# New landing times and durations in a list scheduler's plan, with a third buffer for one tile, in an attention and mixture kernel

## The chip, the cores and the metric

The kernel runs on one core of a Trainium2 chip. TensorE (PE) does the matrix products, ScalarE (ACT) and VectorE (DVE) the elementwise work, SyncE (SP) issues every transfer. The metric is the time of one execution on the device in microseconds, the median of several runs.

## What is computed

```python
def _attn_ref(q, k, v, cap):                      # q, k, v: 4 x 12 heads x 448 x 64
    scores = matmul(q, k.T) / sqrt(64)
    scores = cap * tanh(scores / cap)             # cap = 30
    attn = exp(scores - max)
    attn = attn / (sum(attn) + 1e-09)
    return attn @ v
def _moe_ref(x, w1, w2, w3, w_out):               # x: 1792 x 768, weights in float64
    a = x @ w1
    b = x @ w2
    return (a * b @ w3) @ w_out                   # 768 -> 1024 -> 1024 -> 768
```

The attention's result, its heads laid side by side, is the x of the second part.

## The kernel before

**Attention.** The 48 heads are taken as 24 pairs (`pr`), 128 keys at a time. `plan_S` multiplies q and k on TensorE, ScalarE takes the tanh (L486) and the exp (L489) of 128x896 elements in place in a tile `p`. `plan_V` multiplies `p` with v (L526, L541) into one of two PSUM banks, and `plan_X` adds up the exps for the denominator: for the pairs in `ADDS` (L365) VectorE first adds the tiles of p (L591, L593) and TensorE sums one tile (L608); for the other pairs TensorE sums three. Then ScalarE copies the product out of PSUM into a tile `xf` (task `O`, L674), which frees the bank; the sums go through four transfers and a reciprocal (`R0` L678, `R1`, `R2` L687, `R3` L691), VectorE multiplies `xf` by the result (`N0`, L714), and SyncE stores `xf` to `x_dr` (`N`, L717). The tile `xf` has two buffers in the pool `smp`, so the copy of pair pr waits for the store of pair pr - 2.

**Weights.** They come in float64. A piece of 128x384 is loaded as pairs of words (`raw_w`, `raw_wo`, three buffers, L238), and `Piece` makes a float32 of it: `top` on ScalarE (L253) or VectorE (L246), `low` (L258), `sign` (L261) and `join` (L266) on VectorE. A high and a low part are split off (L272, L275, L313, L316), and each product is made of three passes. `plan_wo`, `plan_w3` and `plan_C` make w3 times w_out (`pc`, L1175) while the attention runs; `plan_W` makes the seven combinations of w1 and w2 that a scheme with seven block products instead of eight needs, and stores them (`w_dr`), since they are read again for the second half of the tokens.

**The second part.** `plan_xprep(r)` loads x for half r of the tokens and makes its combinations (`xs`, tiles `x0B`, `x0T`, `x1B`, `x1T`). `plan_moe(r, m)` multiplies them in eight rounds m (`pab`, L1040), with copies out of PSUM named M1, U, M5 and V (L1009) and sums (L1020), and stores a * b to `u_dr`. Round m of half 0 runs beside the attention from about 210 us on. `plan_out` multiplies the result with w3 times w_out (`m`, L1394).

**What sets the order.** Each `put` adds a task with its engine (and sometimes a second one that may take it), its planned duration, a due time (`key`), the tasks it needs and a `lat`, the time from the issue of a transfer to its landing. `Plan.run` (L94) walks through planned time: for the engine that is free first it takes, of the tasks whose needs are met by then, the one with the smallest due time, and emits its instructions. Loads with `spare` are held back by `SPARE`, 2500 ns more. So these numbers do not change what is computed; they set the order of the instructions on each engine, and which of two engines does a conversion. On the chip each engine then runs its instructions strictly in that order and waits at each one for its operands.

Of the kernel before, what the change touches and what calls it, by code (L numbers as in the profile page):

```python
# [148 lines left out]
def program(  # L149
# [127 lines left out]
    def plan_piece(nm, x, key, lead, first=(), whole=True):  # L277

        n = x.n / PC
        for st, eng, ns, fn, needs, lat, alt in (  # L280
            ("load", "SP", 450, lambda: x.load((rawp, rtp)), (), 3300, ()),
            ("low", "DVE", 75 + 200 * n, x.low, ("load",), 0, ()),
            ("sign", "DVE", 75 + 400 * n, x.sign, ("low",), 0, ()),
            (
                "top", "DVE", 75 + 200 * n, lambda: x.top((rawp, rtp)), ("load",), 0,
                [("ACT", 140 + 272 * n, lambda: x.top_a((rawp, rtp)))] * TOPA,
            ),
            ("join", "DVE", 75 + 400 * n, x.join, ("top", "sign"), 0, ()),
            (
                "high", "ACT", 140 + 272 * n, lambda: x.high_out(nc.scalar.copy), ("join",), 0,  # L290
                [("DVE", 75 + 200 * n, lambda: x.high_out(nc.vector.tensor_copy))],
            ),
            ("out", "DVE", 75 + 400 * n, x.low_out, ("high",), 0, ()),
        )[: 7 if whole else 5]:
            need = [f"{nm}{y}" for y in needs]
            need += list(first) if st == "high" else []
            t = put(f"{nm}{st}", eng, ns, key, fn, need, lat, alt)
            if st == "load":
                t.key -= lead
                t.spare = SPARE  # L300
                raw = plan.tag("raw", NRAW).take(t)
            elif st == "top":
                tt = plan.tag("rt", NRT).take(t)
            if st not in ("high", "out"):
                raw.append(t)
            if st in ("join", "high", "out"):
                tt.append(t)
        return tt
# [53 lines left out]

    LANDS = {0: 3300, 1: 6000, 2: 5000}

    ADDS = [(2,3) if pr>3 else () for pr in range(NPAIR)]  # L365

    def due(pr, i=0):

# [20 lines left out]
    def plan_load(pr):  # L389
        key = due(pr, 0) if pr % 2 else due(pr, 1)  # L390

        def emit():
            raw_t[pr] = qkp.tile([P, QO + KQ], F32, tag="raw", name=f"kq{pr}", bufs=3)
            for c in cuts(pr):
                c = slice(c.start + QO if c.start else 0, (c.stop if c.stop < HK else KQ) + QO)
                nc.sync.dma_start(raw_t[pr][:, c], kq[pr][:, c])

        def emit2():
            v_t[pr] = qkp.tile([P, 7, D], F32, tag="v", name=f"v{pr}")
            nc.sync.dma_start(v_t[pr], v[pr].rearrange("p (m d) -> p m d", m=7))  # L400

        t = put(f"ld{pr}", "SP", 450, key - 12, emit, lat=LANDS.get(pr, 3300))
# [45 lines left out]
    def plan_S(pr, i):  # L448
# [56 lines left out]
        use["p", pr, i] = plan.tag("t" if i else "t0", 5 if i else 2).take(t)  # L505
        if not i:
            use["p", pr + 1, i] = use["p", pr, i]
        t = put(f"E{nm}", "ACT", 935, key, exp, [f"H{nm}"])
        if not i:
            done[f"E{pr + 1}_0"] = t  # L510
        use["p", pr, i].append(t)
# [68 lines left out]
    def plan_X(pr):  # L580
# [89 lines left out]
            nc.scalar.copy(r[0][:, :SH], box[1][:, :SH])  # L670

        def take_values():
            r[1] = smp.tile([P, S], F32, tag="x", name=f"xf{pr}")
            nc.scalar.copy(r[1], pv_t[pr][:, :S])  # L674

        def fold():
# [29 lines left out]
        t = put(f"R2{pr}", "SP", 450, end, unfold, [f"R1{pr}"], 2000)  # L706
        use["z", pr].append(t)
        use["rd", pr] = plan.tag("rd", 2).take(t)
        t = put(f"R3{pr}", "SP", 900, end, spread, [f"R2{pr}"], 2500)
        use["rd", pr].append(t)  # L710
        use["r", pr].append(t)

# [6 lines left out]
        t = put(f"N0{pr}", "DVE", 536, end + 5, scale, [f"R3{pr}", f"O{pr}"])  # L719
        use["r", pr].append(t)  # L720
        use["x", pr].append(t)
        t = put(f"N{pr}", "SP", 450, end + 5, store, [f"N0{pr}"], 2000)
        use["x", pr].append(t)

    def plan_general(pr):

        def emit():
# [47 lines left out]
            for j in range(2):  # L775
                at = slice(j * D, (j + 1) * D)
                for m in range(NCH):
# [5 lines left out]
                        start=(m == 0),  # L783
                        stop=(m == 3),
                    )
            xf = smp.tile([P, S], F32, tag="x", name=f"gx{pr}")
            nc.scalar.copy(xf, pv[:, :S])
            nc.sync.dma_start(x_dr[pr], xf)

# [10 lines left out]

    XORD = (1, 2, 6, 5, 7, 3, 4)
    GATE, NW = 8.0, 4
    RT0, RWIN = (145, 330), (170, 104.0)
    wt, wuse, xt, xuse = {}, {}, {}, {}

    def slot(tag):
# [22 lines left out]
    def plan_W(m):  # L829
# [19 lines left out]
        def split(op, of, needs):  # L849
            i = [x for x in range(7) if LHS[XORD[x]] == op][0]  # L850
            q = m * 7 + i
            j = q // NW
            k = key + 3 + i

            def dst(x):
                if x == 0 and (q, "new") not in wt:
                    wt[q, "new"] = w_new(q)
                return wt[q, "new"][:, x].rearrange("p a b -> p (a b)")

            first = [f"W{(q - q % NW) // 7}_{(q - q % NW) % 7}h"] if q % NW else []  # L860
# [9 lines left out]
            t = put(f"WS{m}_{i}", "SP", 450, k + 4, store, [f"{nm}_{i}l"], 2500)  # L870
            wuse[j].append(t)
            done[f"w0_{m}_{i}"] = done[f"{nm}_{i}l"]

# [17 lines left out]
    def plan_W_again(m):  # L891

        for i in range(7):
            q = (KF + m) * 7 + i

            def load(q=q, i=i):
                nc.sync.dma_start(w_new(q).rearrange("p x a b -> p (x a b)").bitcast(F32), w_dr[m, i])

            p = q - q % NW - KF * 7
            t = put(  # L900
                f"w1_{m}_{i}", "SP", 450, w_key(1, m, i) - 12, load,
                [f"WS{m}_{i}"] + [f"w1_{p // 7}_{p % 7}"] * (q % NW > 0), 3500,
            )
# [11 lines left out]
    def plan_xprep(r):  # L915
# [10 lines left out]
        def load(nm, kt, src, key, needs):  # L926
            x = nm, kt

            def emit():
                tiles[x] = xsp.tile([P, 512], F32, tag="xs", name=f"xs{r}{nm}{kt}")[:, :S]  # L930
                nc.sync.dma_start(tiles[x], src)

            t = put(f"X{r}{nm}{kt}", "SP", 450, key, emit, needs, 2500)
            t.spare = SPARE
            use["xs", r, nm, kt] = plan.tag("xs", NXS).take(t)

# [24 lines left out]
        p0 = r * PH  # L961
        for kt in range(HX):
            a0, b0 = p0 + kt, p0 + HB + kt
            key = max(due(b0, 3) + 14, (140 + 3 * kt) * (r == 0))
            load("a0", kt, x_dr[a0], key - 8, [f"N{a0}"])
            load("b0", kt, x_dr[b0], key - 7, [f"N{b0}"])
            split("B11", "a0", kt, key, [f"X{r}a0{kt}"])
# [3 lines left out]
            def keep(kt=kt):  # L971
                nc.sync.dma_start(t_dr[r, kt], tiles["a0", kt])

            t = put(f"XT{r}{kt}", "SP", 450, key, keep, [f"X{r}T1{kt}"], 2000)
            use["xs", r, "a0", kt].append(t)
        for kt in range(HX):
            a1, b1, b0 = p0 + HX + kt, p0 + HB + HX + kt, p0 + HB + kt
            key = max(due(b1, 3) + 14, (140 + 3 * (3 + 2 * kt)) * (r == 0))
# [13 lines left out]
    def plan_moe(r, m):  # L992
# [170 lines left out]
    def plan_C(n):  # L1163

        for nh in range(2):
# [40 lines left out]
            )  # L1206
            o.append(t)
            ev = plan.tag("ev", NEV).take(t)
            ev.append(put(f"DS{n}_{nh}", "SP", 450, key, store, [f"D{n}_{nh}"], 2000))

    def plan_bt(k, late):

# [3 lines left out]
        def load(nm, a, nh):  # L1216
# [50 lines left out]

    def plan_out(t):

        key = K0 + 14.5 * t - 10 * (t == 0)  # L1270
        ru, box, ob = {}, {}, {}

        if t == 4:
# [5 lines left out]
        def load_quadrant(a, b):  # L1279
            nm = f"A{a + 1}{b + 1}"  # L1280

            def load():
# [152 lines left out]
        def store(name, a, nh, need):  # L1435
# [174 lines left out]
```

## Time and profile before

| | |
|---|---|
| Median of 3 runs | 617.76 us (614.71 to 619.55) |
| The profiled execution | 611.22 us, of which the span is 609.3 us |
| TensorE busy | 558.6 us |
| VectorE busy | 449.9 us |
| ScalarE busy | 327.6 us |
| Mean busy share of the 16 DMA engines | 67.5% for the SyncE queue |

The share of a busy engine is an average over stages with different limits. The kernel has four: a start, the attention with the weight conversion beside it (to about 335 us), the preparation of the second half of x (335 to 424 us), and a tail of matrix products (424 us to the end). A row of the timeline gives the start, the duration, the engine, the line, what is written and read, and, in brackets, the idle time before it and what ended it.

### The profile page before, as it was taken

To read this page: it belongs to the slowest core of one execution; us is meant where nothing else is said; L and a number is where in the kernel's file an instruction comes from. 1 tells how busy PE (TensorE), PEld (TensorE's weight loads), DVE (VectorE), ACT (ScalarE), POOL (GpSimd) and SP (SyncE) were. 2 spreads that over 40 slices of the span, in tenths; PEclk is the share of its full clock that TensorE was granted. 3 is DMA by queue.
4 is the path that set the end of the run, shared out by engine and by line. 5 is a ranking of instruction groups with operands and counts; after the bars stand their busy time and mean duration, and the time that the engine had idled before them with its cause. 6 is when DMAs were issued, how large, how long until landed. Compare 5 with 4: busy or idle time off the path is not lost.

```text
span 609.3 us, 9488 instructions
## 1 busy us (share of the span) xinstructions
PE 558.6 (92%) x3340; PEld 429.5 (70%) x3340; DVE 449.9 (74%) x909; ACT 327.6 (54%) x514; POOL 0.2 (0%) x4
## 2 busy tenths in 40 slices
PE   4999999998999599979899599879999999999995
PEld 2445477665576355646568488768999999999995
DVE  5988998796989779698988779777622388878511
ACT  5998986695677587666873343422212152433200
POOL 0000000000000000000000000000000000000000
PEclk9999999999999799989999889999999999999998
DMA  6668775768688665687777975999886653545211
GB/s 226 198 220 249 235 249 179 231 218 266 203 309 273 203 220 165 199 279 220 274 292 248 333 273 213 362 332 352 273 322 238 237 184 125 169 132 152 63 53 58
DMA packets 80089, 137.45 MB, mean 226 GB/s; under 512 B 13602, under 2 KB 53410, under 8 KB 80034
## 3 DMA queue, kind: packets, MB, share of 16 engines
q1 hardware_dynamic: 80034, 136.77, 67.5%
q8 instruction: 28, 0.46, 0.3%
q14 instruction: 27, 0.22, 0.1%
HBM read 91.67 MB, written 44.98 MB: 224 GB/s over the span
## 4 chain that ended last, share of the span: by engine, by line
PE 46%; DMA 27%; DVE 12%; ACT 8%; SPq 3%; issue 3%; DVEq 0%; ACTq 0%
PE pab L1040 18%; PE m L1394 17%; DMA raw_w<-in_moe_w_dram 5%; DMA r_dr<-z 4%; DMA r<-r_dr 4%; DMA c<-cc_dr 4%; PE pc L1175 4%; PE s L473 3%; ACT p L486 3%; DMA x_dr<-xf 3%; DMA raw_wo<-in_moe_w_out_dram 3%; PE pv L526 2%; ACT p L489 2%; DMA z<-r 2%; DVE wt L316 1%
## 5 line engine op out<-in xcount | busy, mean ns | idle before, releaser
L489 ACT ACTIVATE p<-p,ncap_sb,acap_sb 128x896 f32<-128x896 f32 x84 | 92.1, 1141 | 0.0
L486 ACT ACTIVATE p<-s,tsc_sb 128x896 f32<-128x896 f32 x84 | 81.7, 1015 | 8.2 <-PE s L473 7.8
L1175 PEld LDWEIGHTS pc<-wo,w3t 128*128 128x128 f32 x384 | 65.6, 188 | 12.1 <-issue 6.8
L1175 PE MATMUL pc<-wo,w3t 128*128 128x384 f32 x384 | 73.9, 342 | 0.0
L1040 PE MATMUL pab<-x0T,wt 128*128 128x448 f32 x288 | 64.9, 373 | 7.1 <-ACT M L1009 6.1
L526 PE MATMUL pv<-p,v 128*64 128x448 f32 x288 | 65.6, 571 | 5.5 <-ACT p L489 5.1
L473 PE MATMUL s<-hl 64*128 64x448 f32 x432 | 60.5, 403 | 10.7 <-ACT p L486 6.1
L473 PEld LDWEIGHTS s<-hl 64*128 64x128 f32 x432 | 38.7, 194 | 38.6 <-ACT p L486 14.1
L1040 PEld LDWEIGHTS pab<-x0T,wt 128*128 128x128 f32 x288 | 53.5, 190 | 16.3 <-ACT M L1009 6.5
L1040 PE MATMUL pab<-x1T,wt 128*128 128x448 f32 x288 | 61.8, 366 | 2.7 <-DVE M L1020 2.0
L1394 PE MATMUL m<-bT,ot 128*128 128x384 f32 x336 | 60.7, 334 | 0.0
L1040 PEld LDWEIGHTS pab<-x1T,wt 128*128 128x128 f32 x288 | 53.8, 188 | 7.8 <-DVE M L1020 2.4
L1394 PEld LDWEIGHTS m<-bT,ot 128*128 128x128 f32 x336 | 58.5, 188 | 0.0
L1040 PE MATMUL pab<-x0B,wt 128*128 128x448 f32 x216 | 50.7, 381 | 5.0 <-DVE M L1009 2.2
L1040 PEld LDWEIGHTS pab<-x0B,wt 128*128 128x128 f32 x216 | 40.8, 194 | 13.5 <-DVE M L1009 3.4
L1040 PE MATMUL pab<-x1B,wt 128*128 128x448 f32 x216 | 47.5, 368 | 2.6 <-DVE U L1020 1.0
L1394 PE MATMUL m<-bB,ot 128*128 128x384 f32 x252 | 46.1, 334 | 0.0
L1040 PEld LDWEIGHTS pab<-x1B,wt 128*128 128x128 f32 x216 | 40.1, 188 | 7.6 <-DVE M L1020 1.9
L1394 PEld LDWEIGHTS m<-bB,ot 128*128 128x128 f32 x252 | 43.9, 188 | 0.1
L526 PEld LDWEIGHTS pv<-p,v 128*64 128x64 f32 x288 | 17.4, 139 | 37.3 <-issue 18.7
L253 ACT ACTIVATE t_w<-raw_w 128x384 f32<-128x384 f32 (+1 forms) x44 | 23.9, 552 | 21.1 <-DMA raw_w<-in_moe_w_dram 20.0
L1009 ACT COPY M<-pab 128x448 f32<-128x448 f32 x27 | 14.4, 533 | 36.5 <-PE pab L1040 36.4
(128 smaller groups left out, 717.0 us busy)
## 6 DMA issues: line engine op xcount, KB each, us to landing
w_dr<-wt SPq DMA_DIRECT2D x56, 384.0 KB
wt<-w_dr SPq DMA_DIRECT2D x56, 384.0 KB
raw_w<-in_moe_w_dram SPq DMA_DIRECT2D x48, 384.0 KB
kq<-in_kq_dram SPq DMA_DIRECT2D x23, 450.0 KB
raw_wo<-in_moe_w_out_dram SPq DMA_DIRECT2D x16, 384.0 KB
A<-u_dr SPq DMA_DIRECT2D x24, 256.0 KB
v<-in_v_dram SPq DMA_DIRECT2D x24, 224.0 KB
r<-r_dr SPq DMA_DIRECT2D x48, 112.0 KB
```

Source lines behind the costliest of these rows:

```text
L253: nc.scalar.activation(self.t.bitcast(F32), self.hi.bitcast(F32), AF.Copy, scale=2.0**-112)
L316: nc.vector.tensor_tensor(dst(1), src(), dst(0), op=ALU.subtract)
L473: nc.tensor.matmul(box[0][:, j, :S], lhsT=hl[at, a, S + (i - 1) * P : S + i * P], rhs=hl[at, c, :S], start=(z == 0), stop=(z == 2),)
L486: nc.scalar.activation(p, box[0][:, :, :S], AF.Tanh, scale=tsc_sb)
L489: nc.scalar.activation(p_t[pr, i], p_t[pr, i], AF.Exp, scale=acap_sb, bias=ncap_sb)
L526: nc.tensor.matmul(pv_t[pr][j * D : (j + 1) * D, :S], lhsT=v_t[pr][:, 3 * j + i - 1, :], rhs=p_t[pr, i][:, j, :], start=(i == 1 and not od ...
L1009: cp(ev[name], box[bank][:, :S])
L1040: nc.tensor.matmul(box[bank][:, :S], lhsT=w_op(r, m, i)[:, a, kt, :], rhs=xt[r, i][:, kt, c, :S], start=(new and kt == 0 and z == 0), stop ...
L1175: nc.tensor.matmul(box[0][:, :NH], lhsT=w3t[n][:, a, jt, :], rhs=wo[jt][:, c, ns], start=(jt == 0 and z == 0), stop=(jt == KF - 1 and z == 2),
L1394: nc.tensor.matmul(box[banks[m]][:, :NH], lhsT=ot[q // 3][:, q % 3, a, k, :], rhs=bt[RHS[m]][:, k, c, :], start=(new and k == 0 and z == 0 ...
```

## The change

It replaces numbers in the plan, and gives `xf` a third buffer:

- Landing times (ns): loads of weight pieces 3300 to 4400, of k and q 3300 to 4000, the four transfers of a denominator 2000, 2000 and 2500 to 2700, 2700 and 3400, the store of `xf` 2000 to 4500, the store of a weight combination 2500 to 4500 and its load 3500 to 4500, loads of x 2500 to 4000, stores of `u_dr`, `cc_dr` and the output 2000 to 4500, loads of `cc_dr` 2500 to 4500 and of `u_dr` 2500 to 3500.
- Durations: exp 935 to 1026, `top` on ScalarE from 140 + 272 n to 140 + 320 n.
- `ADDS`: VectorE adds the exps for the pairs above 5 instead of above 3, so pairs 4 and 5 go to TensorE.
- Due times: for the first half of x from 140 to 132.69 us, for the second half's rounds from 330 to 330.67, for the output from 440 to 445.75 (its first tile from 10 to 5 earlier than that), for w_out from 14 + 1.3 n to 14.11 + 1.39 n.

The number of result buffers (`NEV`, L189) is five on both sides.

```diff
@@ plan_piece
-            ("load", "SP", 450, lambda: x.load((rawp, rtp)), (), 3300, ()),
+            ("load", "SP", 450, lambda: x.load((rawp, rtp)), (), 4400, ()),
...
-                [("ACT", 140 + 272 * n, lambda: x.top_a((rawp, rtp)))] * TOPA,
+                [("ACT", 140 + 320 * n, lambda: x.top_a((rawp, rtp)))] * TOPA,
...
-    ADDS = [(2,3) if pr>3 else () for pr in range(NPAIR)]
+    ADDS = [(2,3) if pr>5 else () for pr in range(NPAIR)]
...
@@ plan_S
-        t = put(f"E{nm}", "ACT", 935, key, exp, [f"H{nm}"])
+        t = put(f"E{nm}", "ACT", 1026, key, exp, [f"H{nm}"])
@@ plan_X
-            r[1] = smp.tile([P, S], F32, tag="x", name=f"xf{pr}")
+            r[1] = smp.tile([P, S], F32, tag="x", name=f"xf{pr}", bufs=3)
...
-        use["x", pr] = plan.tag("x", 2).take(t)
-        t = put(f"R0{pr}", "SP", 450, end, fold, [f"Q{pr}"], 2000)
+        use["x", pr] = plan.tag("x", 3).take(t)
+        t = put(f"R0{pr}", "SP", 450, end, fold, [f"Q{pr}"], 2700)
...
-        t = put(f"N{pr}", "SP", 450, end + 5, store, [f"N0{pr}"], 2000)
+        t = put(f"N{pr}", "SP", 450, end + 5, store, [f"N0{pr}"], 4500)
...
@@ plan_xprep
-            key = max(due(b0, 3) + 14, (140 + 3 * kt) * (r == 0))
+            key = max(due(b0, 3) + 14, (132.69 + 3 * kt) * (r == 0))
...
-    K0 = 440
+    K0 = 445.75
```

The plan is made anew, so the order moves. On TensorE the sequence of stages stays, and a pair's last product with v stands within a few tasks of its old place. Conversions that either engine may do change over between ScalarE and VectorE in both directions, and ScalarE's list has one task more than before (514 instead of 513), VectorE's five fewer (871 instead of 876). Three places on ScalarE follow.

At the start of the program, ScalarE's list before, after the split of the first q and k into `hl`, began with the conversion of the first piece of w_out (`t_wo` from `raw_wo`), then the first two tanhs (`p` from `s`) and exps (`p` from `p`):

```order
L419 CAST hl_130<-kq_113 128x576
L419 CAST hl_130<-kq_113 128x256
L253 ACTIVATE t_wo_0_149<-raw_wo_0_124 128x384
L486 ACTIVATE p_1_160<-s_1_142,tsc_sb 128x896
L486 ACTIVATE p_2_164<-s_2_152,tsc_sb 128x896
L489 ACTIVATE p_1_160<-p_1_160,ncap_sb,acap_sb 128x896
L489 ACTIVATE p_2_164<-p_2_164,ncap_sb,acap_sb 128x896
```

In the changed kernel that conversion is gone from ScalarE (VectorE has it, at L246):

```order
L419 CAST hl_130<-kq_113 128x576
L419 CAST hl_130<-kq_113 128x256
L486 ACTIVATE p_1_156<-s_1_142,tsc_sb 128x896
L486 ACTIVATE p_2_160<-s_2_149,tsc_sb 128x896
L489 ACTIVATE p_1_156<-p_1_156,ncap_sb,acap_sb 128x896
L489 ACTIVATE p_2_160<-p_2_160,ncap_sb,acap_sb 128x896
```

The tanhs now stand right behind the split.

At the tanhs of pair 20, some 265 us into the run before, ScalarE had two conversions (`t_w` from `raw_w`) of the combinations of round 3, the copy of pair 19 (`xf`) and of a sum (`r`), and then the tanhs:

```order
L253 ACTIVATE t_w_1_0_2850<-raw_w_1_0_2793 128x384
L313 CAST wt_2845<-t_w_0_0_2732 128x384
L253 ACTIVATE t_w_1_1_2857<-raw_w_1_1_2820 128x384
L674 COPY xf_2867<-pv_2764 128x448
L670 COPY r_2883<-sum_2861 128x224
L486 ACTIVATE p_1_2895<-s_1_2876,tsc_sb 128x896
L486 ACTIVATE p_2_2901<-s_2_2887,tsc_sb 128x896
L489 ACTIVATE p_1_2895<-p_1_2895,ncap_sb,acap_sb 128x896
```

In the changed kernel the same stretch, from the same copy `xf` on, reads:

```order
L674 COPY xf_2863<-pv_2760 128x448
L670 COPY r_2873<-sum_2849 128x224
L253 ACTIVATE t_w_0_1_2875<-raw_w_0_1_2809 128x384
L486 ACTIVATE p_1_2887<-s_1_2865,tsc_sb 128x896
L486 ACTIVATE p_2_2896<-s_2_2877,tsc_sb 128x896
L489 ACTIVATE p_1_2887<-p_1_2887,ncap_sb,acap_sb 128x896
L489 ACTIVATE p_2_2896<-p_2_2896,ncap_sb,acap_sb 128x896
L670 COPY r_2932<-sum_2909 128x224
```

The conversion of the fourth piece (`raw_w_1_1`) has moved behind the four exps of this pair, nine rows below the last shown; that of the second piece (`raw_w_0_1`) stands ahead of the tanhs now.

At the first copy of round 5 (`M_5`, about 348 us into the run before), where the combinations of the second half of x (`x1B`, `x1T`) begin, ScalarE had, with a conversion of round 7's first piece among them:

```order
L1009 COPY V_4_3630<-pab_4_1_3507 128x448
L313 CAST x1B_3633<-xs1a_3606 128x448
L313 CAST x1B_3633<-xs1a_3620 128x448
L313 CAST x1T_3662<-xs1a_3594 128x448
L253 ACTIVATE t_w_0_0_3678<-raw_w_0_0_3640 128x384
L313 CAST x1T_3662<-xs1a_3606 128x448
L1009 COPY M_5_3686<-pab_5_1_3666 128x448
L313 CAST x1B_3715<-xs1a_3684 128x448
```

And in the changed kernel:

```order
L1009 COPY V_4_3624<-pab_4_1_3508 128x448
L253 ACTIVATE t_w_1_0_3632<-raw_w_1_0_3565 128x384
L313 CAST x1B_3659<-xs1a_3618 128x448
L313 CAST x1B_3659<-xs1a_3634 128x448
L1009 COPY M_5_3685<-pab_5_1_3663 128x448
L313 CAST x1T_3691<-xs1a_3608 128x448
L253 ACTIVATE t_w_1_1_3701<-raw_w_1_1_3647 128x384
L313 CAST x1T_3691<-xs1a_3618 128x448
L253 ACTIVATE t_w_0_0_3720<-raw_w_0_0_3661 128x384
L313 CAST x1B_3756<-xs1a_3718 128x448
```

The copy `M_5` has gone ahead of that conversion and of both splits of `x1T`; the conversion of round 6's fourth piece (`raw_w_1_1`), which stood thirteen places ahead of `M_5`, now stands behind it, and its load stands sixteen places later in SyncE's list, behind the store of pair 23.

## Rows read from the trace of the kernel before

**Rows 1.** The page: busy time of each engine, share of the span, instructions.

```profile
PE 558.6 (92%) x3340; PEld 429.5 (70%) x3340; DVE 449.9 (74%) x909; ACT 327.6 (54%) x514; POOL 0.2 (0%) x4
```

**Rows 2.** Stretches: length; PE, PEld, DVE, ACT, POOL busy; clock; DMA share; GB/s.

```profile
0.00:20.00 20.00, 11.99 (x60) 5.32 (x62) 12.69 (x36) 12.43 (x15) 0.20 (x4) 1.00 0.70 236
20.00:80.00 60.00, 56.06 (x442) 27.54 (x441) 52.48 (x115) 55.76 (x78) 0.00 (x0) 1.00 0.73 229
80.00:120.00 40.00, 40.00 (x263) 31.22 (x262) 33.87 (x73) 27.10 (x43) 0.00 (x0) 1.00 0.67 203
200.00:220.00 20.00, 15.19 (x96) 7.71 (x96) 15.98 (x29) 15.50 (x22) 0.00 (x0) 0.83 0.63 192
260.00:280.00 20.00, 16.04 (x111) 9.18 (x107) 17.40 (x36) 12.68 (x19) 0.00 (x0) 0.91 0.81 272
340.00:360.00 20.00, 13.00 (x53) 11.60 (x54) 13.59 (x28) 7.29 (x15) 0.00 (x0) 0.83 0.77 277
424.00:604.00 180.00, 178.99 (x966) 172.74 (x966) 100.58 (x178) 49.52 (x95) 0.00 (x0) 1.00 0.52 171
```

**Rows 3.** Waits of TensorE: us in total, times, longest.

```profile
PE pab L1040 <- ACT M L1009: 7.7, 3, 6.1
...
PE sum L608 <- ACT xf L674: 4.4, 2, 3.8
...
PE sum L608 <- ACT p L486: 4.0, 1, 4.0
```

**Rows 4.** Groups of ScalarE: busy us, mean ns, idle before and what ended it.

```profile
L253 ACT ACTIVATE t_w<-raw_w 128x384 f32<-128x384 f32 (+1 forms) x44 | 23.9, 552 | 21.1 <-DMA raw_w<-in_moe_w_dram 20.0 <-DVE wt L316 0.9
...
L674 ACT COPY xf<-pv 128x448 f32<-128x448 f32 x24 | 12.7, 532 | 19.5 <-DMA x_dr<-xf 16.5 <-PE pv L541 1.9 <-DMA raw_w<-in_moe_w_dram 1.1
```

**Rows 5.** Timeline of the start: TensorE, then two rows of ScalarE.

```profile
5.36 2.23 PE L473 MATMUL s<-hl 64*128 64x448 f32 x10 [0.24 <-DVE hl L423]
...
9.47 0.57 ACT L253 ACTIVATE t_wo<-raw_wo 128x384 f32<-128x384 f32 x1 [4.83 <-DMA raw_wo<-in_moe_w_out_dram]
...
9.92 1.91 ACT L486 ACTIVATE p<-s,tsc_sb 128x896 f32<-128x896 f32 x2
```

**Rows 6.** Timeline, about 202 us: ScalarE, and TensorE behind it.

```profile
201.89 0.53 ACT L674 COPY xf<-pv 128x448 f32<-128x448 f32 x1 [3.57 <-DMA x_dr<-xf]
...
205.77 3.25 PE L526 MATMUL pv<-p,v 128*64 128x448 f32 x8 [2.33 <-ACT p L489]
```

**Rows 7.** Timeline of ScalarE, about 266 us.

```profile
266.52 0.55 ACT L253 ACTIVATE t_w<-raw_w 128x384 f32<-128x384 f32 x1 [3.25 <-DMA raw_w<-in_moe_w_dram]
```

**Rows 8.** Timeline of ScalarE, about 348 us.

```profile
347.61 0.54 ACT L253 ACTIVATE t_w<-raw_w 128x384 f32<-128x384 f32 x1 [4.50 <-DMA raw_w<-in_moe_w_dram]
...
348.52 0.52 ACT L1009 COPY M<-pab 128x448 f32<-128x448 f32 x1
```

**Rows 9.** Chain that ended last: transfers on it, start and length in us.

```profile
58.64 3.34 DMA x_dr<-xf
...
145.81 3.92 DMA raw_w<-in_moe_w_dram
...
280.17 6.16 DMA x_dr<-xf
...
339.61 7.98 DMA raw_w<-in_moe_w_dram
```

**Rows 10.** The three stretches at half clock, columns as in rows 2.

```profile
203.40:210.30 6.90, 4.57 (x20) 1.93 (x18) 6.59 (x12) 4.45 (x7) 0.00 (x0) 0.51 0.83 253
...
268.30:271.70 3.40, 3.00 (x22) 1.51 (x22) 1.93 (x7) 3.40 (x5) 0.00 (x0) 0.50 0.66 243
...
346.80:353.70 6.90, 4.61 (x13) 4.14 (x14) 2.77 (x6) 1.99 (x4) 0.00 (x0) 0.51 0.77 270
```

**Rows 11.** Groups: the sums of exps on TensorE.

```profile
L608 PE MATMUL sum<-a,ones 128*32 128x224 f32 x160 | 12.1, 375 | 8.7 <-ACT p L486 4.0 <-ACT xf L674 3.8 <-DVE a L593 0.9
L608 PE MATMUL sum<-p,ones 128*32 128x224 f32 x96 | 5.4, 357 | 0.6 <-ACT xf L674 0.6
```

More of the change, by code (lines that the diff above doesn't have):

```diff
@@ L400, in emit2 @@
             nc.sync.dma_start(v_t[pr], v[pr].rearrange("p (m d) -> p m d", m=7))
-        t = put(f"ld{pr}", "SP", 450, key - 12, emit, lat=LANDS.get(pr, 3300))
+        t = put(f"ld{pr}", "SP", 450, key - 12, emit, lat=LANDS.get(pr, 4000))
         t.spare = SPARE
@@ L705, in plan_X @@
         use["z", pr].append(t)
-        t = put(f"R2{pr}", "SP", 450, end, unfold, [f"R1{pr}"], 2000)
+        t = put(f"R2{pr}", "SP", 450, end, unfold, [f"R1{pr}"], 2700)
         use["z", pr].append(t)
         use["rd", pr] = plan.tag("rd", 2).take(t)
-        t = put(f"R3{pr}", "SP", 900, end, spread, [f"R2{pr}"], 2500)
+        t = put(f"R3{pr}", "SP", 900, end, spread, [f"R2{pr}"], 3400)
         use["rd", pr].append(t)
@@ L785, in emit @@
                     )
-            xf = smp.tile([P, S], F32, tag="x", name=f"gx{pr}")
+            xf = smp.tile([P, S], F32, tag="x", name=f"gx{pr}", bufs=3)
             nc.scalar.copy(xf, pv[:, :S])
@@ L802, in program @@
     GATE, NW = 8.0, 4
-    RT0, RWIN = (145, 330), (170, 104.0)
+    RT0, RWIN = (145, 330.67), (170, 104.0)
     wt, wuse, xt, xuse = {}, {}, {}, {}
@@ L868, in store @@
                 nc.sync.dma_start(w_dr[m, i], wt[q, "new"].rearrange("p x a b -> p (x a b)").bitcast(F32))
-            t = put(f"WS{m}_{i}", "SP", 450, k + 4, store, [f"{nm}_{i}l"], 2500)
+            t = put(f"WS{m}_{i}", "SP", 450, k + 4, store, [f"{nm}_{i}l"], 4500)
             wuse[j].append(t)
@@ L901, in plan_W_again @@
                 f"w1_{m}_{i}", "SP", 450, w_key(1, m, i) - 12, load,
-                [f"WS{m}_{i}"] + [f"w1_{p // 7}_{p % 7}"] * (q % NW > 0), 3500,
+                [f"WS{m}_{i}"] + [f"w1_{p // 7}_{p % 7}"] * (q % NW > 0), 4500,
             )
@@ L931, in emit @@
                 nc.sync.dma_start(tiles[x], src)
-            t = put(f"X{r}{nm}{kt}", "SP", 450, key, emit, needs, 2500)
+            t = put(f"X{r}{nm}{kt}", "SP", 450, key, emit, needs, 4000)
             t.spare = SPARE
@@ L972, in keep @@
                 nc.sync.dma_start(t_dr[r, kt], tiles["a0", kt])
-            t = put(f"XT{r}{kt}", "SP", 450, key, keep, [f"X{r}T1{kt}"], 2000)
+            t = put(f"XT{r}{kt}", "SP", 450, key, keep, [f"X{r}T1{kt}"], 3500)
             use["xs", r, "a0", kt].append(t)
@@ L977, in plan_xprep @@
             a1, b1, b0 = p0 + HX + kt, p0 + HB + HX + kt, p0 + HB + kt
-            key = max(due(b1, 3) + 14, (140 + 3 * (3 + 2 * kt)) * (r == 0))
+            key = max(due(b1, 3) + 14, (132.69 + 3 * (3 + 2 * kt)) * (r == 0))
             load("a1", kt, x_dr[a1], key - 8, [f"N{a1}"])
@@ L1026, in emit @@
                 nc.sync.dma_start(u_dr[m, :, b * S : (b + 1) * S], ev[name])
-            t = put(f"U{b}_{m}", "SP", 700, key - 2, emit, [f"e{x}_{nm}" for x in needs], 2000)
+            t = put(f"U{b}_{m}", "SP", 700, key - 2, emit, [f"e{x}_{nm}" for x in needs], 4500)
             use["ev", nm, name].append(t)
@@ L1137, in plan_wo @@
         nm = f"O{jt}_{nh}"
-        key = 14 + (jt * 2 + nh) * 1.3
+        key = 14.11 + (jt * 2 + nh) * 1.39
         plan_piece(
@@ L1208, in plan_C @@
             ev = plan.tag("ev", NEV).take(t)
-            ev.append(put(f"DS{n}_{nh}", "SP", 450, key, store, [f"D{n}_{nh}"], 2000))
+            ev.append(put(f"DS{n}_{nh}", "SP", 450, key, store, [f"D{n}_{nh}"], 4500))
     def plan_bt(k, late):
@@ L1219, in emit @@
                 nc.sync.dma_start(tiles[nm], cc_dr[a * HF + k, nh])
-            t = put(f"b{nm}_{k}_{late}", "SP", 450, key - 8, emit, [f"DS{a * HF + k}_{nh}"], 2500)
+            t = put(f"b{nm}_{k}_{late}", "SP", 450, key - 8, emit, [f"DS{a * HF + k}_{nh}"], 4500)
             t.spare = SPARE
@@ L1268, in plan_out @@
     def plan_out(t):
-        key = K0 + 14.5 * t - 10 * (t == 0)
+        key = K0 + 14.5 * t - 5 * (t == 0)
         ru, box, ob = {}, {}, {}
@@ L1293, in load_quadrant @@
                 f"q{t}{nm}", "SP", 800, key, load,
-                [f"U{t0 // S}_{m}" for t0, _ in at[a] for m in range(b * HF, (b + 1) * HF)], 2500,
+                [f"U{t0 // S}_{m}" for t0, _ in at[a] for m in range(b * HF, (b + 1) * HF)], 3500,
             )
@@ L1442, in emit @@
                     x += n
-            x = put(f"w{t}{name}", "SP", 450, key - 5, emit, [need], 2000)
+            x = put(f"w{t}{name}", "SP", 450, key - 5, emit, [need], 4500)
             use[name, t].append(x)
```

## The prediction

> **What bounds the kernel now.** I read the page's busy times first. TensorE is busy for 558.6 of 609.3 us, so 50.7 us of it are idle; VectorE has 74%, ScalarE 54% [rows 1]. No single engine is full, so the question is where TensorE stands and for whom. The busy times by stretch answer the first half: from 80 to 120 us and from 424 to 604 us TensorE is practically without a gap (40.00 of 40, 178.99 of 180), and what it does there the change leaves alone. From 20 to 80 us TensorE has 56.06 of 60 us and ScalarE 55.76, which leaves little to win. The large gaps lie in three stretches of 20 us: 4.8 us at 200, 4.0 us at 260 and 7.0 us at 340 [rows 2]; the reader should see that each of these three also has a granted clock below 1.00, and the others have not. The first 20 us add 8.0 us.
>
> The waits of TensorE give the second half: in the three stretches the longest are for copies and tanhs on ScalarE, 3.8, 4.0 and 6.1 us [rows 3]. ScalarE is not slow there; it stands itself. It runs its list in order, and it stood 20.0 us at conversions of weight pieces that had not landed and 16.5 us at `xf` copies whose buffer was still being stored [rows 4]. So the kernel loses its time by work that was queued behind a transfer which the plan believed to be there. The plan has 3.3 us for a weight piece and 2.0 us for a store of `xf`; the chain of waits has 3.92 to 7.98 us and 3.34 to 6.16 us [rows 9].
>
> **The change, part by part.** All sums are made against the profiled execution, 611.22 us; the median of the three timed runs, 617.76 us, is 1.0107 times that, and the result is scaled by it at the end.
>
> *The start.* ScalarE stood 4.83 us at the first w_out piece and began its tanhs at 9.92 us, although TensorE had begun the products for them at 5.36 us [rows 5]. In the changed list the conversion is no longer ahead of them (first place in the order). The group of ten products at 5.36 took 2.23 us and holds the last four of the first tanh's six; four tenths of it are 0.9 us, so the first tanh can start at about 6.3 us, 3.6 us earlier. VectorE still waits for that piece before the second pair's low part, which is not needed until ScalarE has done four tanhs and four exps. I take 3.5 us, with 0 and 3.6 as bounds. Until 80 us ScalarE is close to full and after it TensorE is full, so a start that is earlier passes through.
>
> *The third buffer of xf.* With it a copy waits for the store of three pairs earlier, and the 24 pairs are spread over 335 us, some 14 us apart, so the store is long done. What TensorE saw of the 16.5 us is 4.4 us in two waits for `xf` [rows 3] and the 2.33 us that it waited for the exp behind the copy at 201.89 us [rows 6]: 6.7 us. Bounds: 0, if the next thing in line is just as late, and 16.5 us.
>
> By the Trainium skill ("DMA: Bandwidth & Descriptors", section "Anatomy of one DMA") a transfer takes about 2.0 us plus its bytes over 436 GB/s, which for the 224 KB of `xf` would be an estimate of 2.5 us. The old 2000 ns would then be nearly right, 4500 ns too long, and the third buffer would save nothing. The page's fit is for another way of issuing; the trace here has 3.34 and 6.16 us [rows 9] and goes against it.
>
> *The conversion at 266 us.* The fourth piece of round 3 held ScalarE for 3.25 us [rows 7], and TensorE lost 4.0 us to the tanh behind it [rows 3]. It has moved behind the four exps (second place). Gain 4.0 us, lower bound 0, since the second piece of the round now stands ahead of these tanhs.
>
> *The conversion at 348 us.* It held ScalarE for 4.50 us, the copy of round 5 came after it [rows 8], and TensorE lost 6.1 us [rows 3]. The copy now stands ahead (third place). Gain 6.1 us, lower bound 0.
>
> *The clock.* After each of these three stalls the trace has a stretch at 1.2 GHz instead of 2.4, in which TensorE was busy for 4.57, 3.00 and 4.61 us [rows 10], 12.2 us together. At 2.4 GHz that work takes half, so 6.1 us come back if the stalls in front of them go; 0 if they don't.
>
> *The adds of pairs 4 and 5.* They go from VectorE to TensorE. VectorE loses four adds, which I leave out of the sum. TensorE sums three tiles instead of one: 5.4 us over four pairs against 12.1 over twenty [rows 11], 1.35 against 0.60 us, so 0.75 us a pair and 1.5 us in all. This lies in the stretch in which TensorE has 4 us of 60 free, so between 0 and 1.5 us shows; I take 1.5 as a cost.
>
> *The rest.* The longer durations of exp and `top` and the due times have no price of their own, only an effect on the order. Of the idle time of TensorE outside the start, the three stretches and the tail, 50.7 - 8.0 - 15.8 - 1.0, or 26 us in many small waits, the better numbers should save some; nothing shows how much, so I take 2 us of the bounds 0 and 26. Conversions that change engine go in both directions and nearly cancel. Both sides have five result buffers, so there is nothing to count for these. The tail has TensorE full, and the order of its products is the same but for the last round of half 1.
>
> *The sum.* The stalls and the clock are 6.7 + 4.0 + 6.1 + 6.1 = 22.9 us. They will not all stay away. The new numbers, 4.4 us for a weight piece, 4.5 for a store, are still in the middle of what was measured, not at its upper end, so a piece that takes 7.98 us holds its engine again; and VectorE, which must finish the same weights in less time, is at 52.5 of 60 us in the first stretch [rows 2]. I take half, 11.4 us, as what remains won; that is a choice between the bounds 0 and 22.9. So 3.5 + 11.4 + 2 - 1.5 = 15.4 us are saved: 611.2 - 15.4 = 595.8 us, and times 1.0107 that is 602 us.
>
> **The rivals.** *Everything named stays won*: 3.5 + 22.9 + 2 - 1.5 = 26.9 us, 584.3 us, scaled 591. For it speaks that each of the stalls has one named cause, and that the order or the buffer removes just that. Against it speaks that the engine next in line can be nearly as late: at 202 us TensorE had two waits in a row, first for the copy, then for the exp behind it [rows 3, 6].
>
> *The stalls move.* Only the start is won, 3.5 + 2 - 1.5 = 4 us: 607.2, scaled 614, which can't be told from no change. VectorE would be the place: in the stretch at 260 it is busy for 17.40 of 20 us and the DMA engines for 0.81 [rows 2], so products of the weights come no sooner and TensorE waits for them instead of for tanhs. This is also what comes out if the landing times do nothing at all but shift work around. By the Trainium skill's rule cited above only the third buffer's 6.7 us would fall away, half of which is in the likeliest sum: 12.0 us instead of 15.4, scaled 606.
>
> *Slower: the weights of rounds 6 and 7 come too late.* TensorE takes the rounds in a fixed order. In the change the load of round 6's fourth piece stands behind the store of pair 23, sixteen places later, and its conversion behind the first copy of round 5 (third place), and round 7 follows it. Three of a round's seven products, and one that is the piece itself, need that piece. If each of the two rounds has TensorE stand as the stretch from 340 to 360 us does, that is 7.0 us idle and 2.3 us of half clock [rows 2, 10], 9.3 us each, 18.6 together; with only the start won it gives 607.2 + 18.6 = 625.8, scaled 632. It decides against the change from the point where these waits exceed the gains by 6 us. Against it speaks that in the order all 63 products of round 5 stand between that copy and round 6's first, so much of the delay is slack.
>
> **How the numbers follow.** The likeliest case, half of the stalls won, gets 0.52; everything won 0.17; the stalls move 0.21; slower 0.10. About 1% is what can be told from no change here, 611.6 to 623.9 us. The first two cases lie below it, and a little of the third: faster 0.71, within 1% 0.20, slower 0.09. The range reaches from a little beyond the second case, 587, to beyond the third, 618; that leaves out the slower case and a gain of more than 5%. The likeliest case alone has 595 to 609.
>
> **What would show it.** Right: the first tanh starts near 6.3 us; no `xf` copy waits for `x_dr`; the wait of ScalarE for weight pieces falls clearly below 20 us; the three stretches at half clock are gone or fewer; the tail still takes 180 us and begins near 409 us instead of 424. Wrong: VectorE's waits for landings, or TensorE's waits for `wt`, have grown by what ScalarE's have lost; or TensorE stands between 335 us and the tail for longer than before, in rounds 5 to 7 of half 0.

## The result and the profile after

The changed kernel takes 591.19 us (median of 4 runs, 586.48 to 594.39) against 616.24 us before (4 runs as well), a ratio of 0.9624 with a 95% interval of 0.9506 to 0.9741. The forecast was 602 us in a range of 587 to 618, and the rival in which everything named stays won had 591. The profiled execution took 590.31 us, its span is 588.5 us.

The busy times by stretch, with the columns of [rows 2]; the last row is the tail, which begins some 20 us sooner:

```profile
0.00:20.00 20.00, 15.37 (x108) 7.25 (x110) 12.97 (x36) 15.43 (x18) 0.20 (x4) 1.00 0.78 253
20.00:80.00 60.00, 56.68 (x451) 27.50 (x448) 52.25 (x121) 56.15 (x78) 0.00 (x0) 1.00 0.72 232
200.00:220.00 20.00, 18.15 (x127) 9.48 (x126) 19.91 (x37) 19.47 (x27) 0.00 (x0) 1.00 0.80 242
260.00:280.00 20.00, 20.00 (x141) 13.20 (x141) 19.27 (x41) 16.07 (x22) 0.00 (x0) 1.00 0.83 293
340.00:360.00 20.00, 18.04 (x86) 15.62 (x85) 19.28 (x41) 8.57 (x18) 0.00 (x0) 1.00 0.83 297
404.00:584.00 180.00, 177.68 (x961) 171.53 (x959) 97.51 (x171) 49.34 (x96) 0.00 (x0) 1.00 0.53 172
```

In the stretches at 200, 260 and 340 us TensorE now has 18.15, 20.00 and 18.04 of 20 us, where it had 15.19, 16.04 and 13.00, and all three are at full clock. But look at the third number as well: VectorE is at 19.91, 19.27 and 19.28 us there, and had 15.98, 17.40 and 13.59. It works almost without a pause where it used to stand.

The waits of TensorE (us in total, times, longest). None of the three of [rows 3] is left at its size; a new one is for `x1T`, a combination of the second half of x:

```profile
PE pab L1040 <- ACT x1T L313: 3.5, 1, 3.5
...
PE sum L608 <- ACT xf L674: 0.8, 1, 0.8
```

The groups of ScalarE that answer to [rows 4], and, from the list by line, VectorE's multiplication of `xf` by the reciprocal sums (L714) with its idle time:

```profile
L253 ACT ACTIVATE t_w<-raw_w 128x384 f32<-128x384 f32 (+1 forms) x48 | 25.9, 546 | 14.3 <-DMA raw_w<-in_moe_w_dram 13.6 <-DVE wt L316 0.5
...
L674 ACT COPY xf<-pv 128x448 f32<-128x448 f32 x24 | 12.7, 529 | 13.3 <-PE pv L541 8.2 <-DMA raw_w<-in_moe_w_dram 2.8 <-PE pv L526 2.1
```

```profile
L714 DVE TENSOR_TENSOR xf<-xf,r 128x448 f32<-128x448 f32 x24 | 14.9, 620 | 4.8 <-DMA r<-r_dr 4.8
```

No copy of `xf` waits for a store any more, and weight pieces hold ScalarE for 13.6 us instead of 20.0. The last row is one that the prediction did not use; before, it read:

```profile
L714 DVE TENSOR_TENSOR xf<-xf,r 128x448 f32<-128x448 f32 x24 | 14.9, 620 | 17.4 <-DMA r<-r_dr 13.1 <-issue 4.3
```

VectorE stood there 17.4 us and now stands 4.8 us. The experiments ask which of these three changes counts.

Where the time was won can be read from that same multiplication. The last of its 24 begins at 334.3 us before and at 312.9 us after, 21.4 us sooner. From there to the tail it takes 89.7 us before and 91.1 us after. So all of the gain of the profiled executions (20.8 us, from a span of 609.3 to one of 588.5) lies in the attention, and the preparation of the second half of x is no shorter than it was.

### The profile page after: what moved, and what is told of

Read it like the earlier page. It is cut to its first block, busy times and chain, and to the rows that moved or that the text cites. A ratio compares the mean times of both kernels' runs of the same rounds, so it can differ in the third digit from the quotient of the medians.

```text
span 588.5 us, 9547 instructions
## 1 busy us (share of the span) xinstructions
PE 558.5 (95%) x3372; PEld 431.7 (73%) x3372; DVE 444.4 (76%) x904; ACT 329.2 (56%) x515; POOL 0.2 (0%) x4
## 4 chain that ended last, share of the span: by engine, by line
PE 58%; DVE 16%; DMA 14%; ACT 5%; SPq 3%; issue 2%; DVEq 0%
PE pab L1040 25%; PE m L1394 17%; PE pc L1175 5%; PE pv L526 4%; PE s L473 4%; DMA raw_w<-in_moe_w_dram 3%; DMA raw_wo<-in_moe_w_out_dram 2%; DMA xs1t<-t_dr 2%; DMA r_dr<-z 2%; DMA r<-r_dr 2%; DMA wt<-w_dr 2%; ACT p L489 2%; DVE wt L316 2%; ACT p L486 1%; DVE hl L423 1%
## 5 line engine op out<-in xcount | busy, mean ns | idle before, releaser
L1175 PEld LDWEIGHTS pc<-wo,w3t 128*128 128x128 f32 x384 | 65.4, 188 | 12.3 <-issue 10.0
L1040 PE MATMUL pab<-x1T,wt 128*128 128x448 f32 x288 | 63.4, 372 | 3.8 <-ACT x1T L313 3.5
L526 PE MATMUL pv<-p,v 128*64 128x448 f32 x288 | 62.5, 552 | 1.3 <-ACT p L489 1.1
L1040 PE MATMUL pab<-x1B,wt 128*128 128x448 f32 x216 | 49.3, 381 | 2.2 <-DVE U L1020 2.2
L1040 PEld LDWEIGHTS pab<-x1B,wt 128*128 128x128 f32 x216 | 42.7, 198 | 6.1 <-DVE U L1020 2.6
L253 ACT ACTIVATE t_w<-raw_w 128x384 f32<-128x384 f32 (+1 forms) x48 | 25.9, 546 | 14.3 <-DMA raw_w<-in_moe_w_dram 13.6
```

Of the source, the lines that this page charges most:

```text
L253: nc.scalar.activation(self.t.bitcast(F32), self.hi.bitcast(F32), AF.Copy, scale=2.0**-112)
L526: nc.tensor.matmul(pv_t[pr][j * D : (j + 1) * D, :S], lhsT=v_t[pr][:, 3 * j + i - 1, :], rhs=p_t[pr, i][:, j, :], start=(i == 1 and not od ...
L1040: nc.tensor.matmul(box[bank][:, :S], lhsT=w_op(r, m, i)[:, a, kt, :], rhs=xt[r, i][:, kt, c, :S], start=(new and kt == 0 and z == 0), stop ...
L1175: nc.tensor.matmul(box[0][:, :NH], lhsT=w3t[n][:, a, jt, :], rhs=wo[jt][:, c, ns], start=(jt == 0 and z == 0), stop=(jt == KF - 1 and z == 2),
```

## The experiments

Each kernel ran beside the kernel before on the same chip; ratios are to it.

**The third buffer alone, in the old order.**

```diff
-            r[1] = smp.tile([P, S], F32, tag="x", name=f"xf{pr}")
+            r[1] = smp.tile([P, S], F32, tag="x", name=f"xf{pr}", bufs=3)
```

> The kernel before with a third buffer for xf in the pool alone; the plan still counts two, so every engine's order is the same as before, row by row. Theory of the prediction: the 16.5 us that ScalarE stood at xf copies for stores go, and TensorE gets back the 4.4 us at the sums, and part of what follows the copy; 4 to 10 us, a ratio of 0.985 to 0.993. Rival (the buffer does nearly everything of the 3.8%): 0.96 to 0.97. Rival (the next thing is just as late, or only the order counts): 0.995 to 1.005.

614.78 us, 0.9969 (0.9928 to 1.0011). The order is the same on every engine. ScalarE's waits for the stores are all gone, and the time is not clearly different. The timeline of ScalarE at the place of [rows 6] shows why:

```profile
201.57 0.53 ACT L674 COPY xf<-pv 128x448 f32<-128x448 f32 x1
206.22 0.57 ACT L313 CAST x0T<-xs0t 128x448 fp32r<-128x448 f32 x1 [4.12 <-DVE xs0t L334]
206.69 1.90 ACT L486 ACTIVATE p<-s,tsc_sb 128x896 f32<-128x896 f32 x2
```

The copy waits for nothing, and the next instruction waits 4.12 us for VectorE. VectorE in turn, in the same stretch, and TensorE behind both:

```profile
198.04 0.63 DVE L714 TENSOR_TENSOR xf<-xf,r 128x448 f32<-128x448 f32 x1 [0.74 <-DMA r<-r_dr]
...
205.56 0.62 DVE L334 TENSOR_TENSOR xs0t<-xs0b,xs0t 128x448 f32<-128x448 f32 x1 [3.71 <-DMA xs0b<-x_dr]
```

```profile
209.66 3.26 PE L526 MATMUL pv<-p,v 128*64 128x448 f32 x8 [6.55 <-ACT p L489]
```

So TensorE still stands, for 6.55 us in one piece. The stall was handed to the next in line, a load of x.

**The changed kernel with two buffers.** In the pool and in the plan:

```diff
-            r[1] = smp.tile([P, S], F32, tag="x", name=f"xf{pr}", bufs=3)
+            r[1] = smp.tile([P, S], F32, tag="x", name=f"xf{pr}")
-        use["x", pr] = plan.tag("x", 3).take(t)
+        use["x", pr] = plan.tag("x", 2).take(t)
```

> The changed kernel with two buffers for xf again, in the pool and in the plan. If buffer and landing times add up, it is 4 to 10 us slower than the changed kernel, a ratio to before of 0.97 to 0.98. If the plan, which now counts 4.5 us for the store, can order around two buffers, it stays at 0.96 to 0.965. If the buffer does nearly everything, about 0.99 to 1.00.

595.39 us, 0.967 (0.9615 to 0.9725), between the first two forecasts. The intervals of this and of the changed kernel overlap, so the loss without the buffer, some 3 us by the two ratios, is not shown. Two waits of this run matter further down: ScalarE's for weight pieces and VectorE's at L714 are near their old sizes, 21.3 and 14.2 us, although it keeps most of the gain.

```profile
L253 ACT ACTIVATE t_w<-raw_w 128x384 f32<-128x384 f32 (+1 forms) x47 | 25.6, 554 | 21.6 <-DMA raw_w<-in_moe_w_dram 21.3 <-DVE wt L316 0.2
...
L714 DVE TENSOR_TENSOR xf<-xf,r 128x448 f32<-128x448 f32 x24 | 14.9, 619 | 14.2 <-DMA r<-r_dr 14.2
```

**The new landing times alone**, all fifteen, and nothing else of the change. The list of the change leaves out one of the fifteen: the store of the copy of T1 (`t_dr`), 2000 to 3500 ns.

> The kernel before with the new landing times alone: two buffers, old durations of exp and top, old adds, old due times. Theory: the landing times carry the larger part, since they move work behind transfers: 0.97 to 0.98. If the buffer does nearly everything: 0.99 to 1.00. If any new order gives a few per cent by luck, it is anywhere between 0.97 and 1.02, and does not fit with the two runs on the buffer.

590.52 us, 0.9602 (0.9551 to 0.9654), more than its own forecast: the whole gain, with two buffers, the old durations, adds and due times. Its wait at L714 is 4.8 us, as in the changed kernel.

**A change of no meaning.**

```diff
-            ("load", "SP", 450, lambda: x.load((rawp, rtp)), (), 3300, ()),
+            ("load", "SP", 450, lambda: x.load((rawp, rtp)), (), 3330, ()),
```

> The kernel before with the landing time of weight loads at 3330 instead of 3300 ns: a change of no meaning, which still reshuffles a part of the order. It measures how far a new order alone moves the time. Theory of the prediction: within 1% of before (0.99 to 1.01). Rival (the gain is the luck of an order): a difference of 2% or more in either direction.

615.91 us, 0.9991 (0.9952 to 1.003), although a part of the order is new. A reshuffle alone gave nothing here; it is one sample, and a smaller reshuffle than the others: counted in the traces by line and tile names, 804 of VectorE's 909 instructions keep their old sequence, against 564 in the changed kernel.

**The change without the landing times.** Third buffer, durations, adds and due times stay.

> The changed kernel with the old landing times: what the third buffer in plan and pool, the durations, the adds of pairs 4 and 5 and the due times do without them. If the landing times carry everything: 0.99 to 1.005. If the parts add up to something beside them: 0.975 to 0.985.

603.57 us, 0.9793 (0.9718 to 0.9867). So these do something, 2%, but on top of the landing times they add nothing that can be measured. Which of the four does it wasn't separated. It also means that a gain of 2% does not by itself speak for landing times.

**The landing time of the weight pieces alone**, 3300 to 4400 ns:

```diff
-            ("load", "SP", 450, lambda: x.load((rawp, rtp)), (), 3300, ()),
+            ("load", "SP", 450, lambda: x.load((rawp, rtp)), (), 4400, ()),
```

> The kernel before with the landing time of the weight pieces alone at 4400 ns. ScalarE stood 20.0 us at these pieces, and two of the three large stalls hang on them, so if the prediction's two conversions are the cause: 0.975 to 0.985, about half of the 4%. If it takes all the landing times together: 0.99 to 1.0.

613.95 us, 0.9955 (0.9921 to 0.9988). This was the test of the prediction's two conversions, and they fail it. Its groups:

```profile
L253 ACT ACTIVATE t_w<-raw_w 128x384 f32<-128x384 f32 (+1 forms) x47 | 25.1, 545 | 12.6 <-DMA raw_w<-in_moe_w_dram 11.8 <-DVE wt L316 0.7
```

```profile
L714 DVE TENSOR_TENSOR xf<-xf,r 128x448 f32<-128x448 f32 x24 | 14.9, 620 | 18.1 <-DMA r<-r_dr 17.7 <-issue 0.4
```

ScalarE's wait for weight pieces is even shorter than in the changed kernel, 11.8 us, and hardly anything is gained. VectorE stands at L714 for 18.1 us, as before. The stall at 348 us has only moved: TensorE stands 6.68 us in one piece a little earlier, and the chain ahead of it runs from a denominator's last transfer over L714 to a load of x.

```profile
327.41 5.08 DMA r<-r_dr
...
332.86 0.64 DVE xf L714
...
334.84 5.06 DMA xs1a<-x_dr
```

```profile
344.41 5.58 PE L1040 MATMUL pab<-x0B,wt 128*128 128x448 f32 x18 [6.68 <-DVE U L1020]
```

This order is new to a larger part than that of the run below with the denominators alone (604 of VectorE's 909 instructions keep their old sequence, there 668), so a large reshuffle did not bring a few per cent by itself here either.

**The landing times of the stores alone** (`xf`, weight combinations, the copy of T1, `u_dr`, `cc_dr`, the output).

> The kernel before with the landing times of the stores alone (xf, weight combinations, u_dr, cc_dr, the copy of T1, the output). Two buffers for xf: if the plan, told of 4.5 us, orders around the store, ScalarE's 16.5 us at xf copies shrink to under 6 and the time is 0.98 to 0.99. If a stall passes to the next in line as with the third buffer: 0.995 to 1.005.

604.38 us, 0.9803 (0.9729 to 0.9876). That is what the first of its two forecasts says. The waits of `xf` copies shrink to 2.9 us, but the wait at L714 does too, to 12.5 us, so this run doesn't tell them apart. With the first run, in which the same waits were gone in the old order for 0.3%, most of these 2% should come from the new order and not from the buffer's wait.

**The denominators' transfers and the loads of x, k and q and the rest alone.**

> The kernel before with the remaining landing times alone: k and q, the transfers of the denominators, the loads of x, of weight combinations, of cc_dr and u_dr. VectorE stood 13.1 us at the denominators' last transfer and ScalarE behind x (the next in line after the xf copy at 202 us is a split of x). If those are what a stall passes to: 0.98 to 0.99. If weight loads carry nearly all: 0.995 to 1.005.

591.2 us, 0.957 (0.9498 to 0.9642), outside both forecasts: again the whole gain, with ScalarE's waits for `xf` stores still at 12.3 us and the start as late as before (first tanh at 10.20 us). The wait at L714 is 5.7 us. This gave the theory of the next three runs, the "new theory" of their forecasts.

**The three transfers of a denominator alone.** (The third step is issued as two transfers, one for each head of the pair; the list of the change counts four.)

```diff
-        t = put(f"R0{pr}", "SP", 450, end, fold, [f"Q{pr}"], 2000)
+        t = put(f"R0{pr}", "SP", 450, end, fold, [f"Q{pr}"], 2700)
...
-        t = put(f"R2{pr}", "SP", 450, end, unfold, [f"R1{pr}"], 2000)
+        t = put(f"R2{pr}", "SP", 450, end, unfold, [f"R1{pr}"], 2700)
...
-        t = put(f"R3{pr}", "SP", 900, end, spread, [f"R2{pr}"], 2500)
+        t = put(f"R3{pr}", "SP", 900, end, spread, [f"R2{pr}"], 3400)
```

> The kernel before with the landing times of the three transfers of a denominator alone: 2700, 2700 and 3400 instead of 2000, 2000 and 2500 ns. New theory: VectorE, not ScalarE, is where the time goes; it stands in order at the multiplication that waits for the third transfer (17.4 us at L714 before, about 5 in the three kernels at 0.96), and the weights and x behind it come late. Then these three numbers bring most of the gain, 0.96 to 0.975, and the wait at L714 falls below 8 us. Rival (the loads of x carry it): 0.99 to 1.00, and the wait at L714 falls all the same. Rival (the luck of an order): no relation between the wait at L714 and the time.

601.07 us, 0.9753 (0.969 to 0.9815). Three numbers bring about two thirds of the gain, just at the upper edge of the forecast. Its groups of VectorE and ScalarE:

```profile
L714 DVE TENSOR_TENSOR xf<-xf,r 128x448 f32<-128x448 f32 x24 | 14.9, 620 | 7.5 <-DMA r<-r_dr 6.9 <-issue 0.5
```

```profile
L253 ACT ACTIVATE t_w<-raw_w 128x384 f32<-128x384 f32 (+1 forms) x44 | 23.9, 549 | 19.8 <-DMA raw_w<-in_moe_w_dram 19.6 <-DVE w3t L275 0.2
...
L674 ACT COPY xf<-pv 128x448 f32<-128x448 f32 x24 | 12.7, 533 | 18.3 <-DMA x_dr<-xf 14.9 <-PE pv L541 1.9 <-DVE wt L316 1.0
```

Both waits of ScalarE that the prediction priced stand almost at their old size, 19.6 and 14.9 us, and the kernel is 15 us faster. VectorE's wait at L714 is 9.9 us shorter. By stretch, the gain is not at the first of the three stalls:

```profile
200.00:220.00 20.00, 14.91 (x98) 7.53 (x96) 15.63 (x29) 16.23 (x23) 0.00 (x0) 0.91 0.71 231
...
260.00:280.00 20.00, 18.64 (x123) 12.49 (x119) 18.73 (x38) 14.53 (x20) 0.00 (x0) 1.00 0.76 256
...
340.00:360.00 20.00, 19.33 (x90) 16.52 (x90) 17.95 (x39) 8.18 (x17) 0.00 (x0) 1.00 0.95 324
```

TensorE has 14.91 of 20 us at 200 (15.19 before), 18.64 at 260 (16.04) and 19.33 at 340 (13.00).

**The other loads of that group alone** (k and q, x, weight combinations, `cc_dr`, `u_dr`).

> The kernel before with the other landing times of that group alone: k and q, x, weight combinations, cc_dr, u_dr. New theory: 0.985 to 1.00, and the wait at L714 stays above 12 us. Rival (the loads of x carry it): 0.96 to 0.975.

607.58 us, 0.9884 (0.9823 to 0.9945); the wait at L714 is 14.9 us. About as the new theory has it.

**The changed kernel with the denominators' times set back.**

> The changed kernel with the landing times of the denominators' three transfers set back. New theory: the wait at L714 goes back above 10 us and the time to 0.975 to 0.985. Rival (everything else carries it too): 0.955 to 0.967.

604.83 us, 0.9801 (0.9753 to 0.985): half of the gain is lost, with the other twelve landing times, the buffer and the early start all there. The wait at L714 is longer than in the kernel before:

```profile
L714 DVE TENSOR_TENSOR xf<-xf,r 128x448 f32<-128x448 f32 x24 | 14.9, 622 | 25.0 <-DMA r<-r_dr 25.0
```

**Longer still**: weight loads 5400, denominators 3300, 3300 and 4400, x 5500, `cc_dr` 7000 ns.

> The changed kernel with landing times at the upper end of what was measured: weight loads 5400, the denominators 3300, 3300 and 4400, x 5500, cc_dr 7000 ns. If what is left of the waits is still work behind transfers, as in the two waits of TensorE for x behind its own copy in memory, 0.945 to 0.957. If the plan then starts things too late, 0.965 to 0.98.

588.68 us, 0.9557 (0.9515 to 0.9599). The lowest median of all, but its interval overlaps that of the changed kernel, so it is not shown to be better.

## Why the prediction was right, and where not

**The frame held.** The kernel lost time to work that stood behind a transfer which the plan believed to be there; told the longer times, the plan moved it. The landing times alone make the whole gain, no run was measurably slower than before, and the tail stayed as long as it was. The sum of 15.4 us came out at about 25 by the medians (20.9 by the profiled executions), inside the range. That it did is in part luck: tried alone, the terms that make up most of the sum did not bring what they were priced at, and one that was put at almost nothing brought most. That 591 us is also the number of the rival in which everything named stays won is luck for the same reason.

**The wrong engine was priced.** The step that failed is the one from the waits of TensorE to ScalarE: "ScalarE is not slow there; it stands itself", and from there to weight pieces and stores. That was the last link of the chain, not the first. The chain of waits of the kernel before, read further back from the copy at 201.89 us, has

```profile
191.56 3.68 DMA r<-r_dr
...
195.27 0.63 DVE xf L714
...
195.93 5.89 DMA x_dr<-xf
...
201.89 0.53 ACT xf L674
```

ahead of the stall at 268 us, again a transfer of a denominator and VectorE behind it,

```profile
254.11 2.67 DMA r<-r_dr
...
257.79 0.63 DVE xf L714
258.42 0.48 DVE t_w L334
```

and, ahead of the one at 349 us,

```profile
329.56 4.66 DMA r<-r_dr
...
334.34 0.62 DVE xf L714
...
335.36 2.20 DMA xs1a<-x_dr
...
339.61 7.98 DMA raw_w<-in_moe_w_dram
```

All three run through a denominator's last transfer and the multiplication at L714, and differ behind it: first comes the store of `xf`, then conversions on VectorE, then a load of x, more work on VectorE and the weight piece that SyncE issued after it. VectorE itself stood only 0.76 us at the first of them and 4.26 us at the second:

```profile
195.27 0.63 DVE L714 TENSOR_TENSOR xf<-xf,r 128x448 f32<-128x448 f32 x1 [0.76 <-DMA r<-r_dr]
...
257.79 0.63 DVE L714 TENSOR_TENSOR xf<-xf,r 128x448 f32<-128x448 f32 x1 [4.26 <-issue]
```

The plan's own numbers fit this: the three transfers were planned with 2.0, 2.0 and 2.5 us, in a row, so their errors would add up at one instruction, while the chain has 2.31 to 6.62 us for the second of them alone and 1.87 to 5.63 us for the third. The prediction has no term of its own for these three numbers; their waits fell under its "many small waits", which it put at 2 us. Alone they bring 15 us, so this is the mis-sized term.

**How far that is shown.** That the denominators' three numbers carry 2.5% alone, and that undoing them costs half of the gain, is measured. That the time goes by way of VectorE standing at L714 is argued, and the total of that wait does not measure it. It is 14.2 us in the changed kernel with two buffers, at 0.967, and 14.9 us with the other loads alone, at 0.9884; it is 25.0 us with the denominators' times set back, at 0.9801, and 17.4 us in the kernel before. No run moved this multiplication alone in an otherwise old order, as the first run did with the buffer.

**Term by term.** *The start*: the first tanh begins at 6.53 us, 3.39 us sooner (3.5 forecast):

```profile
6.53 2.13 ACT L486 ACTIVATE p<-s,tsc_sb 128x896 f32<-128x896 f32 x2 [1.88 <-PE s L473]
```

That it "passes through" is not borne out. The run with the weight pieces alone has the same early start and is at 0.9955; the run with denominators and x has the late start and is at 0.957. *The third buffer*: 3.4 us counted, 1.9 us measured with an interval that includes nothing. The rival that the next in line is as late was right for this part. *The two conversions*: 5.1 us counted, 2.8 us measured for all weight pieces and the start together. Both moved as said, and TensorE's waits there are gone in the changed kernel. But the stage in which the second of them lay takes 91.1 us instead of 89.7, so its 6.1 us do not show there: TensorE is idle for 10.8 us instead of 15.2, but 13.7 us of the stage are at half clock instead of 6.9. *The clock*: 6.1 us at most, half of it counted, and nothing came in the profiled executions. The changed kernel has three stretches at 1.2 GHz too, in other places:

```profile
331.60:335.00 3.40, 3.40 (x11) 3.01 (x10) 2.74 (x6) 1.96 (x5) 0.00 (x0) 0.50 0.85 261
369.10:372.60 3.50, 3.50 (x11) 3.13 (x11) 3.50 (x8) 0.80 (x2) 0.00 (x0) 0.51 1.01 375
379.40:386.20 6.80, 5.29 (x14) 4.30 (x15) 4.26 (x8) 2.07 (x4) 0.00 (x0) 0.50 1.05 395
```

TensorE was busy for 12.19 us in them, against 12.18 us in those of [rows 10]. *The adds*: TensorE's sums take 18.6 us (10.5 and 8.1) instead of 17.5, so 1.1 us where 1.5 was said. Whether that reaches the end wasn't tried alone.

**The rivals.** For the stores of `xf` the chain before has 3.34 to 6.16 us [rows 9], and giving the plan 4.5 us instead of 2.0 for the stores alone made the kernel 2% faster. The Trainium skill ("DMA: Bandwidth & Descriptors", "Anatomy of one DMA") gives about 2.0 us and the bytes over 436 GB/s, for transfers issued by GpSimd; for 224 KB that is an estimate of 2.5 us. The traces here, of transfers issued by SyncE, are above it. The slower rival, round 6 coming too late, did not happen: in rounds 6 and 7, from about 338 to 367 us in the changed kernel, the longest wait of TensorE is 1.04 us. What did come is a smaller relative of it in the first round of the second half, where TensorE waited 3.5 us for `x1T`, which needs a copy of a combination that is stored to memory and loaded again. In the chain of the changed kernel these loads took

```profile
362.51 5.10 DMA xs1t<-t_dr
...
372.95 6.66 DMA xs1t<-t_dr
```

with 4.0 us in the plan. That may give back a part of the gain. The run with 5.5 us for them is not shown to be better, so how much remains open.

**What stays open.** The parts do not add up: denominators 2.5%, stores 2.0, other loads 1.2 and weight pieces 0.5 make about 6%, all together 4.0. Each number remakes the whole plan, so the parts need not add up. How the 2% without landing times come about wasn't tried apart.

## What to carry to other kernels

When an engine that runs its list in order stands at an instruction, follow the chain back through the engines to the transfers ahead of it, and price those too; a wait at the end of the chain can be taken away without any gain, as with the buffer here, where the next in line was just as late. Several short transfers in a row, each planned a little too short, can matter more than a long one: here they were worth 2.5%, the error at the long weight loads 0.5%. And a stall that looks expensive in one place is best tested by an edit that leaves the order as it is; with the buffer that took away a false cause. A total of waits is no such test: two of the kernels here kept most or half of the gain with the wait near or above its old size.

## What the runs showed of the hardware

The stretches at half clock did not go with the stalls; they moved. In the kernel before they begin in or shortly behind gaps of TensorE of 3.83, 3.96 and 6.08 us. In the changed kernel the gaps ahead of the first two are 2.31 and 2.22 us, and the clock fell to 1.2 GHz all the same; the third begins in a gap of 3.47 us. Rows of the timeline of TensorE after:

```profile
330.36 2.71 PE L1040 MATMUL pab<-x0T,wt 128*128 128x448 f32 x9 [2.31 <-DVE U L1009]
...
368.85 5.50 PE L1040 MATMUL pab<-x1B,wt 128*128 128x448 f32 x18 [2.22 <-DVE U L1020]
```

On the chain of the kernel before, the transfers that carry 3.5 KB (`r_dr` from `z`) took 2.31 to 6.62 us, about as long as stores of 224 KB, which had 3.34 to 6.16 us. For these few, which the chain picks for being late, the size said little about when they land.
